# Late stages of an attention and gated-unit backward kernel: VectorE in program order, input-gradient rows ended over two head groups, O*wo rows reordered

## The chip, the cores and the metric

The kernel runs on one core of a Trainium2 chip. The metric is device time in microseconds (us). The kernel before takes 4983.85 us, the median of four runs (4983.04 to 5001.55).

The engines are TensorE (PE in the profile; its weight loads are PEld), VectorE (DVE), ScalarE (ACT), GpSimd (POOL) and SyncE (SP). SP computes nothing: it issues transfers. POOL computes a little and issues the other transfers. Each engine works through its own list of instructions in order, and waits at an instruction until the semaphores it names have come.

## The reference

One forward pass and its gradients with respect to eight inputs. With S = 2048 rows, D = 576 columns, H = 32 heads of width 128, F = 4608:

```
xn  = layernorm(x)
q   = xn @ wq, per head;  p = softmax(q k^T / sqrt(128));  o = p v
s   = concat(o) @ wo
g   = silu( (sigmoid(xn @ w_gate) * (xn @ w_up)) @ w_down )
out = x + s * g
```

`jax.vjp` of this with a given `grad_out` yields the gradients of x, k, v, wq, wo, w_gate, w_up and w_down. Everything is bfloat16 in memory. The kernel writes nine outputs: `out` (out_0), the gradient of x (out_1), of k and v (out_2, out_3), wq (out_4), wo (out_5), w_gate, w_up (out_6, out_7) and w_down (out_8).

## The kernel before

Rows are handled in NT = 16 tiles of 128. A first part computes the layer norm, the gated unit and the silu, and attention walks over the heads, forward and backward. Both are untouched. Attention leaves in HBM the attention output (`on2_d`), the gradient of q (`dq2_d`), and, turned the wrong way round, the gradients of k and v (`kvT_d`). The gated unit left `a_d` (the sigmoid) and `h_d` (the product). What follows are the late stages, within one `tc.manual_schedule`. In it SP and POOL issue in the order of the program text. The instructions of TensorE, ScalarE and VectorE are put in an order ahead of the run by a planner, with estimated costs; at run time each engine follows its fixed list.

**O*wo.** For each of the 16 row tiles, `load_oT` (line 584, SP) brings the attention output of all heads in, transposed, to one of three places `oTs` (tiles KQ, xnT and xn_all in the profile). `mm(st, heads)` adds 32 heads' products with the rows of wo (line 957, TensorE). The wo rows lie in tiles that attention has finished with; three of these (Kn, Vn, dOn) become free last, and their heads are `h_late`, the others `h_early`. `close(st)` copies the sums out (ScalarE), multiplies by the loaded rows dsg and g2b and adds xb (VectorE, lines 969 to 972), stores out_0 (POOL) and asks for the row three further on. `turn_do(st)` turns the tile doB on TensorE (line 915) into doBT, through a PSUM tile and copies on ScalarE and VectorE. The first three rows run their early heads first, then the late heads of each.

**Blocks.** F is cut into 18 blocks of 256 columns (`for fb`). Two tiles, ah0 and ah1, hold a and h of this block and the next in turn (loads on POOL, line 895). The loop over row pairs computes dh = doB * w_down^T (line 1092, TensorE, two PSUM buffers). From dh come nbl = (a-1)*h (line 1093, VectorE; it needs only a and h), du_blk = dh*a (line 1094, VectorE), ndh = -dh (line 1096, ScalarE) and dg_blk = ndh*nbl (line 1097, VectorE). duT and dgT are turned by SP (line 1047). Then come six sums over all rows by `accumulate` (line 997): two for out_8 (copied to dwd by ScalarE) and two each for out_7 and out_6 (copied to dwT, turned by SP, line 1121). Last, for 16 rows, `dx_row` (line 1052) gives the block's share of the input gradient, which VectorE adds to dxn (line 1130).

**The k and v gradients** are turned along the way: `kv_turn` issues one 512 KB transpose on SP (line 1038) into one of two buffers kvn, `kv_store` its store on POOL (line 1044). There are 64 of them. The blocks do three each, so 54; the head groups do the rest.

**Head groups.** The 32 heads form eight groups of four (`for hg`). A group loads the next one's `onb` and `dqb` (POOL, lines 1026 and 1029), turns its slice of wq (SP, line 1179; the tile shares memory with wdT) and dqb (SP, into dqbT), and does four pairs of sums: for out_4 (copied to dqT, turned by SP, line 1202) and for out_5 (copied to dwo, line 40, stored by POOL, line 1209). Then `dx_more(st)` gives the group's share of the input gradient for each row, four products each, and VectorE adds it to dxn (line 1222). In the last group the rows are instead ended: `finish(st, acc)` does five VectorE operations (tot, junk, m, nb, t; lines 1156 to 1163), one ScalarE operation on t (line 1164), and on POOL the addition of `grad_out`'s row to give dx (line 1166) and its store. All 16 rows do this in the last group, spread between its sums from the second on. The sums share four PSUM buffers.

Of the kernel before, what the change touches and what calls it, by code (L numbers as in the profile page):

```python
# [9 lines left out]
bf = mybir.dt.bfloat16  # L10
f32 = mybir.dt.float32
# [55 lines left out]
def kernel(  # L67
# [814 lines left out]
    with late("pc") as pc, late("pcf") as pcf, \  # L882
            tc.manual_schedule(engines={mybir.EngineType.SP, mybir.EngineType.Pool}):
# [21 lines left out]
        with late("c1l3", 4) as ldp3, late("c1s", 2) as sb, \  # L905
# [4 lines left out]
            def turn_do(st):  # L910
                pt = pst.tile([P, 8, P], bf, name="pt", tag="tr")
# [27 lines left out]
            loads = {}  # L939
            for st in range(1, R0):  # L940
                load_oT(oTs[st], st)
            loads[0] = row_loads(0)
# [33 lines left out]
            for st in range(R0):  # L976
                mm(st, h_early)
            for st in range(NT):
# [5 lines left out]
                while len(pend_tr) > 1:  # L984
                    st_ = pend_tr.pop(0)
                    turn_do(st_)
                mm(st, h_late if st < R0 else h_early + h_late)
                close(st)
            for st_ in pend_tr:
                turn_do(st_)  # L990
# [66 lines left out]
        with late("b1b") as blk, late("b1t", 3) as tmpp, late("b1o", 2) as outp, \  # L1057
# [4 lines left out]
            kdw = 0  # L1062
            for fb in range(NFB):
# [22 lines left out]
                for st in range(0, NT, G2):  # L1086
                    sp_ = slice(st, st + G2)
                    dh = ps.tile([P, G2, FB], f32, name="dh")
# [4 lines left out]
                    nc.vector.scalar_tensor_tensor(nbl[:, sp_, :], a_blk[:, sp_, :], 1.0, h_blk[:, sp_, :], op0=ALU.subtract, op1=ALU.mult)  # L1093
# [5 lines left out]
                    if e % NTQ == 0:  # L1099
                        for k in range(2):  # L1100
                            turn_rows(dugT[k], dug[k], e - NTQ, e, FBT)
                kv_store()
# [3 lines left out]
                for fl in range(FBT):  # L1106
                    dwd = outp.tile([P, D], bf, name="dwd")
                    accumulate(psa.tile([P, WD], f32, name="acc"), h_blk, doB, slice(fl * P, (fl + 1) * P), dwd)
# [5 lines left out]
                for (blk_, out_, nm) in ((du_blk, out_7, "dwu"), (dg_blk, out_6, "dwg")):  # L1114
                    stg_ = outp.tile([P, DT, FB], bf, name=nm)
                    for fl in range(FBT):
# [3 lines left out]
                        accumulate(psa.tile([P, WD], f32, name="acc"), blk_, xn_all, lcols, dwT)  # L1120
                        nc.sync.dma_start_transpose(stg_[:, :, lcols], dwT[:])
                    store_T(out_, fcols, stg_)
                kv_turn(blk)
                for st in range(NT):
                    acc = psa.tile([P, WD], f32, name="acc")
# [3 lines left out]
                    else:  # L1129
                        nc.vector.tensor_tensor(dxn[:, st, :], acc[:, :D], dxn[:, st, :], op=ALU.add)  # L1130
                kv_store()

        with late("c2w") as wp, late("c2b") as blk, late("c2s", 2) as sb, late("c2ps", 4, space=PSUM) as ps:
            dqTs = padded(wp, 2, "dqT")
            onqs = [(onb0, dqb_at.get(0)), tuple(blk.tile([P, NT, HC], bf, name=nm)[:] for nm in ("onb", "dqb"))]
            if not dqb_at:
                onqs[0] = (onb0, carve(ah0[:], "p a t f -> p (a t f)", NT, HC))
                load_dq(onqs[0][1], 0)
            dqbT = blk.tile([P, NT * HG, P], bf, name="dqbT")

            def dx_more(st):
                acc = ps.tile([P, WD], f32, name="acc")
                dx_row(acc, st, [(dqbT[:, st * HG + hl, :], wqT[:, hl, :]) for hl in range(HG)])
# [112 lines left out]
```

## Time and profile before

| what | us |
|---|---|
| median of four runs | 4983.85 |
| the profiled execution's own time | 4995.39 |
| its span, first to last instruction | 4993.6 |
| TensorE busy in it | 4845.4 |
| VectorE busy | 2794.1 |
| ScalarE busy | 2475.6 |
| POOL busy | 864.5 |

The profiled execution is a single one and is 11.5 us above the median. Views of the profile give, for an instruction, its start and duration in us, the engine, the line of the kernel, the operation, what it writes and reads (out<-in), and in square brackets how long its engine was idle before it and what ended that wait. "SPq" stands for a transfer that SP issues; its duration there is that of the issue, and a merged row (x4) spans several. In the view of windows each engine's busy time in a stretch is followed by its number of instructions; the last three columns are the granted TensorE clock (1 is full), the busy share of the 16 DMA engines (which can exceed 1 where transfers overlap) and the GB moved per second. A row of waits names the waiting instruction, what it waited for, and the total, the number and the longest.

### The profile page before, as it was taken

The page shows a single profiled execution, that of the slowest core. Times are in us where ns is not written, and L with a number is a line of the kernel's source. Part 1 is how long each engine was busy: PE and PEld are TensorE (multiplying, and loading weights), DVE is VectorE, ACT ScalarE, POOL GpSimd, SP SyncE. Part 2 cuts the span into 40 slices and gives each one's busy share as a digit, 9 for nine tenths or more (in the row PEclk, how much of TensorE's full clock was granted, in tenths as well). Part 3 has the DMA queues.
Part 4 walks back from the last instruction along what each step waited for, and adds up shares of the span by engine and source line. Part 5 has one row for each costly group of instructions (what it writes and reads, how often), then busy time and mean ns, then how long its engine had stood idle before and what let it go on. Part 6 is the DMA issues. An engine that isn't in the chain of part 4 may idle for free.

```text
span 4993.6 us, 100884 instructions
## 1 busy us (share of the span) xinstructions
PE 4845.4 (97%) x40269; PEld 2895.8 (58%) x41029; DVE 2794.1 (56%) x6546; ACT 2475.6 (50%) x4228; POOL 864.5 (17%) x1344
## 2 busy tenths in 40 slices
PE   8999999999999999999999999999999999998998
PEld 4445666666666666666666666665555555554554
DVE  4544665666666666566566666666334545452225
ACT  4422766766766766766666676676221111111011
POOL 3322111111111111111111111111221111111113
PEclk9999999999999999999999999999999999999999
DMA  7887999999999999999999999999998889889974
GB/s 260 272 207 170 224 227 226 228 230 224 226 234 226 221 228 234 220 230 223 228 221 240 220 224 237 224 223 228 221 226 192 208 190 206 194 208 204 252 206 122
DMA packets 3045876, 1097.09 MB, mean 220 GB/s; under 512 B 2949585, under 2 KB 2953810, under 8 KB 3045394
## 3 DMA queue, kind: packets, MB, share of 16 engines
q1 hardware_dynamic: 2946626, 771.07, 82.3%
q0 software_dynamic: 98160, 318.85, 20.1%
q8 instruction: 322, 5.28, 0.4%
q14 instruction: 160, 1.31, 0.1%
q10 hardware_dynamic: 608, 0.59, 0.0%
HBM read 175.31 MB, written 177.93 MB: 71 GB/s over the span
## 4 chain that ended last, share of the span: by engine, by line
PE 85%; DMA 7%; DVE 3%; issue 2%; SPq 1%; POOL 1%; ACT 1%; DVEq 0%; POOLq 0%; ACTq 0%
PE acc L683 18%; PE acc L744 17%; PE acc L997 12%; PE dp L706 8%; PE sp L636 8%; PE acc L215 5%; DMA ah<-h_d 3%; PE acc L1052 3%; PE u_ps L450 3%; PE g_ps L448 3%; PE acc L533 2%; PE acc L957 2%; DMA kvn<-kvT_d 1%; DMA PT<-Pq 1%; PE acct L145 1%
## 5 line engine op out<-in xcount | busy, mean ns | idle before, releaser
L654 ACT ACTIVATE Pq<-sp 128x1024 bf16<-128x1024 f32 x1024 | 1047.0, 1023 | 270.5 <-PE sp L636 227.6
L709 DVE SCALAR_TENSOR_TENSOR Pq<-dp,negdelta,Pq 128x1024 bf16<-128x1024 f32 x512 | 654.8, 1279 | 42.9 <-PE dp L706 42.8
L712 ACT ACTIVATE t<-dp,negdelta 128x1024 bf16<-128x1024 f32 x512 | 567.2, 1114 | 215.5 <-PE dp L706 165.7
L683 PEld LDWEIGHTS <-dST 128*128 128x128 bf16 x8192 | 507.3, 98 | 148.9 <-DMA dST<-Pq 8.3
L706 PE MATMUL dp<-VT,dOT 128*128 128x512 bf16 x1919 | 581.2, 379 | 2.4
L683 PEld LDWEIGHTS <-PT 128*128 128x128 bf16 x8192 | 500.0, 98 | 142.0 <-DMA PT<-Pq 24.3
L636 PE MATMUL sp<-KQ 128*128 128x512 bf16 x1858 | 567.8, 379 | 2.2 <-ACT Pq L654 2.1
L683 PE MATMUL acc<-Kn,dST 128*128 128x128 bf16 x8192 | 556.3, 219 | 5.4 <-DMA dST<-Pq 3.3
L683 PE MATMUL acc<-Vn,PT 128*128 128x128 bf16 x8192 | 543.0, 219 | 17.2 <-DMA PT<-Pq 14.6
L744 PE MATMUL acc<-Pq,dOn 128*128 128x512 bf16 x1983 | 528.2, 379 | 10.2 <-issue 0.2
L713 DVE TENSOR_TENSOR Pq<-t,Pq 128x1024 bf16<-128x1024 bf16 x512 | 354.4, 692 | 313.2 <-ACT t L712 305.8
L744 PE MATMUL acc<-Pq,Qn 128*128 128x512 bf16 x2013 | 522.9, 379 | 5.0
L1130 DVE TENSOR_TENSOR dxn<-acc,dxn 128x576 f32<-128x576 f32 x272 | 206.0, 757 | 388.9 <-PE acc L1052 388.9
L724 ACT ACTIVATE dq_n<-acc,rsc 128x128 bf16<-128x128 f32 x512 | 187.5, 366 | 329.5 <-PE acc L683 308.0
L744 PEld LDWEIGHTS <-Qn 128*128 128x128 bf16 x2048 | 200.1, 98 | 240.0
L744 PEld LDWEIGHTS <-dOn 128*128 128x128 bf16 x2048 | 199.0, 98 | 234.5 <-issue 1.1
L1096 ACT ACTIVATE ndh<-dh 128x512 bf16<-128x512 f32 x144 | 86.0, 597 | 407.9 <-DVE du_blk L1094 407.8
L706 PEld LDWEIGHTS <-dOT 128*128 128x128 bf16 x2048 | 178.8, 98 | 124.5 <-issue 12.4
L636 PEld LDWEIGHTS <-KQ 128*128 128x128 bf16 x2048 | 179.0, 98 | 123.8 <-issue 3.1
L641 DVE TENSOR_REDUCE rs_all<-rsp 128x1 f32<-128x2 f32 x512 | 78.4, 153 | 306.3 <-ACT Pq L654 294.9
L677 POOL DMA_DIRECT2D on_d<-o_n x128 | 97.1, 759 | 793.0 <-DVE junk L695 460.0
L1222 DVE TENSOR_TENSOR dxn<-acc,dxn 128x576 f32<-128x576 f32 x112 | 84.8, 757 | 263.0 <-PE acc L1052 263.0
(206 smaller groups left out, 6834.5 us busy)
## 6 DMA issues: line engine op xcount, KB each, us to landing
out_dram<-kvn POOLq DMA_DIRECT2D x64, 512.0 KB, 4.5
ah<-a_d POOLq DMA_DIRECT2D x18, 1024.0 KB, 8.6
ah<-h_d POOLq DMA_DIRECT2D x18, 1024.0 KB, 10.9
h_d<-h_row POOLq DMA_DIRECT2D x64, 256.0 KB, 3.3
a_d<-a_row POOLq DMA_DIRECT2D x64, 256.0 KB, 3.7
x_all<-in_A_k_cache_dram SPq DMA_DIRECT2D x64, 256.0 KB, 3.6
on_d<-o_n POOLq DMA_DIRECT2D x128, 128.0 KB, 4.8
kvT_d<-KQ POOLq DMA_DIRECT2D x32, 512.0 KB, 4.9
```

What stands on the lines that cost most here:

```text
L215: nc.tensor.matmul(av[:, :CH], lhsT=w[:, i, :], rhs=srcT[:, i, cs], start=(i == 0), stop=(i == DT - 1))
L636: nc.tensor.matmul(sp[:, c * CH:(c + 1) * CH], lhsT=hs.QT[:, qt * P:(qt + 1) * P], rhs=hs.KT[:, hf * HW_ + c * CH: hf * HW_ + (c + 1) * CH ...
L654: nc.scalar.activation(Pq[:, hsl], sp[:], AF.Exp, scale=SCALE, accum_out=hs.rsp[:, hf:hf + 1])
L683: nc.tensor.matmul(hs.acc[:, 0, :], lhsT=T[:, kt, :], rhs=rhs[:, kt, :], start=(kt == 0), stop=(kt == NT - 1))
L706: nc.tensor.matmul(dp[:, c * CH:(c + 1) * CH], lhsT=hs.dOT[:, qt * P:(qt + 1) * P], rhs=hs.VT[:, hf * HW_ + c * CH: hf * HW_ + (c + 1) * C ...
L709: nc.vector.scalar_tensor_tensor(Pq[:, hsl], dp[:], hs.negdelta[:, qt:qt + 1], Pq[:, hsl], op0=ALU.add, op1=ALU.mult)
L712: nc.scalar.activation(t[:], dp[:], AF.Identity, bias=hs.negdelta[:, qt:qt + 1], scale=1.0)
L713: nc.vector.tensor_tensor(Pq[:, hsl], t[:], Pq[:, hsl], op=ALU.mult)
L724: nc.scalar.activation(hs.dq_n[:, qt % G4, :], hs.acc[:, 0, :], AF.Copy, scale=hs.rsc[:, qt:qt + 1])
L744: nc.tensor.matmul(self.acc, lhsT=self.nat[:, qt, :], rhs=self.slabs[qt][:, cs], start=(qt == self.lo), stop=(qt == self.hi - 1))
L997: nc.tensor.matmul(acc[:, n0:n0 + nn], lhsT=lhs[:, st, cols], rhs=rhs[:, st, n0:n0 + nn], start=(st == 0), stop=(st == NT - 1))
L1130: nc.vector.tensor_tensor(dxn[:, st, :], acc[:, :D], dxn[:, st, :], op=ALU.add)
```

## The change

VectorE joins SP and POOL in the list of engines that follow the program text. With that, the text itself is rearranged:

- **O*wo.** Row 0's loads come first. Before the transposes of rows 1 and 2, POOL copies one element from one of those loads (g2b for row 1, xb for row 2) into the target, so that the transpose waits for it. Two rows, not three, run their early heads ahead; row 2's follow the closing of row 0. The last turns of doB go to the next stage, into the loop of the first block, where they use a PSUM buffer of the sums.
- **Blocks.** nbl is computed within the loop only in the first block; otherwise it is made for the next block behind the loop. A fourth kv transpose and store come per block: one transpose and one store behind the turns of dwu, one transpose behind those of dwg. A loop behind the blocks would do what is left.
- **Head groups.** They do no kv work. In the last but one group (`early`), the first eight rows are ended for both groups at once: they take eight products, four with dqbT and wqT and four with a second pair, dqbT2 and wqT2, turned from the last group's data. These rows are spread from that group's fourth sum on. Its other eight rows are added to dxn as before. The last group ends the other eight rows and turns only their part of dqb.
- **finish.** The addition of `grad_out`'s row moves from POOL to VectorE.

```diff
-            tc.manual_schedule(engines={mybir.EngineType.SP, mybir.EngineType.Pool}):
+            tc.manual_schedule(engines={mybir.EngineType.SP, mybir.EngineType.Pool, mybir.EngineType.DVE}):
...
-            def turn_do(st):
-                pt = pst.tile([P, 8, P], bf, name="pt", tag="tr")
+            def turn_do(st, pt):
...
+            loads[0] = row_loads(0)
             for st in range(1, R0):
+                nc.gpsimd.tensor_copy(oTs[st][0:1, 0, 0:1], loads[0][st % 3][0:1, 0:1])
                 load_oT(oTs[st], st)
-            loads[0] = row_loads(0)
...
-            for st in range(R0):
+            for st in range(R0 - 1):
                 mm(st, h_early)
...
-                mm(st, h_late if st < R0 else h_early + h_late)
+                mm(st, h_late if st in accs_of else h_early + h_late)
                 close(st)
-            for st_ in pend_tr:
-                turn_do(st_)
+                if st == 0 and R0 > 1:
+                    mm(R0 - 1, h_early)
...
+            def make_nbl(src, sl):
+                nc.vector.scalar_tensor_tensor(nbl[:, sl, :], src[:, 0, sl, :], 1.0, src[:, 1, sl, :], op0=ALU.subtract, op1=ALU.mult)
...
+                    while fb == 0 and pend_tr and (len(pend_tr) > 2 or st + 2 * G2 >= pend_tr[0]):
+                        turn_do(pend_tr.pop(0), psa.tile([P, WD // P * 2, P], bf, name="pt", tag="acc"))
...
-                    nc.vector.scalar_tensor_tensor(nbl[:, sp_, :], a_blk[:, sp_, :], 1.0, h_blk[:, sp_, :], op0=ALU.subtract, op1=ALU.mult)
+                    if fb == 0:
+                        make_nbl(ahb, sp_)
...
+                if fb + 1 < NFB:
+                    for st in range(0, NT, G2):
+                        make_nbl(nxt, slice(st, st + G2))
                 kv_store()
                 kv_turn(blk)
...
                     store_T(out_, fcols, stg_)
-                kv_turn(blk)
+                    kv_turn(blk)
+                    if nm == "dwu":
+                        kv_store()
...
+            while kv_left or kv_wait:
+                kv_turn(blk)
+                kv_store()
...
+            NTE = NT // 2 if NHG > 1 else 0
             dqbT = blk.tile([P, NT * HG, P], bf, name="dqbT")
+            dqbT2 = blk.tile([P, max(1, NTE) * HG, P], bf, name="dqbT2")
+            wqT2 = blk.tile([P, HG, D], bf, name="wqT2")
...
-            def dx_more(st):
+            def dx_more(st, both=False):
                 acc = ps.tile([P, WD], f32, name="acc")
-                dx_row(acc, st, [(dqbT[:, st * HG + hl, :], wqT[:, hl, :]) for hl in range(HG)])
+                terms = [(dqbT[:, st * HG + hl, :], wqT[:, hl, :]) for hl in range(HG)]
+                if both:
+                    terms += [(dqbT2[:, st * HG + hl, :], wqT2[:, hl, :]) for hl in range(HG)]
+                dx_row(acc, st, terms)
...
-                nc.gpsimd.tensor_tensor(dx[:], t[:], gots.pop(st)[:], op=ALU.add)
+                nc.vector.tensor_tensor(dx[:], t[:], gots.pop(st)[:], op=ALU.add)
...
+                early = hg == NHG - 2
+                ends = list(range(NTE)) if early else list(range(NTE, NT)) if final else []
...
-                if not final:
-                    kv_turn(blk)
                 nc.sync.dma_start_transpose(wqT, A_wq[:, cols])
-                for a in range(0, NT, NQ):
-                    turn_rows(dqbT, dqb, a, a + NQ, HG)
+                for a in range(NTE if final else 0, NT, NQ):
+                    turn_rows(dqbT, dqb, a, min(a + NQ, NT), HG)
+                if early:
+                    nc.sync.dma_start_transpose(wqT2[:], A_wq[:, (hg + 1) * HC:(hg + 2) * HC])
+                    turn_rows(dqbT2, onqs[(hg + 1) % 2][1], 0, NTE, HG)
...
+                wait_n = min(4 if early else 2, nsteps - 2)
+                todo_rows = list(ends)
...
+                def ends_rows():
+                    if todo_rows and step_n >= wait_n:
+                        for _ in range(-(-len(todo_rows) // max(1, nsteps - step_n - final))):
+                            if todo_rows:
+                                st = todo_rows.pop(0)
+                                finish(st, dx_more(st, early))
+                                if st + 2 <= ends[-1]:
+                                    load_got(st + 2)
...
-                    kv_store()
-                    for st in range(NT):
+                    for st in range(len(ends), NT):
                         acc = dx_more(st)
                         nc.vector.tensor_tensor(dxn[:, st, :], acc[:, :D], dxn[:, st, :], op=ALU.add)
-            while kv_left or kv_wait:
-                kv_turn(blk)
-                kv_store()
+                while todo_rows:
+                    step_n = nsteps
+                    ends_rows()
```

## The prediction

> **What bounds the kernel now.** I read the shares first, then the late stages as windows, the waits in them, and the timeline at each long wait.
>
> ```profile
> PE 4845.4 (97%) x40269; PEld 2895.8 (58%) x41029; DVE 2794.1 (56%) x6546; ACT 2475.6 (50%) x4228; POOL 864.5 (17%) x1344
> ```
> TensorE (PE) sets the time: a gain has to come from its idle time, about 148 us of the span. Attention (to about 3536 us) is not edited. The windows of the rest are, in order: O*wo, all feed-forward blocks, head groups 0, 1 and 6, and the last group, 7.
>
> ```profile
> core 0: us, PE busy (x) PEld busy (x) DVE busy (x) ACT busy (x) POOL busy (x), PEclk, DMA share, GB/s
> 3535.80:3676.00 140.20, 131.28 (x1078) 69.74 (x1100) 36.97 (x61) 17.78 (x45) 38.88 (x69) 0.98 0.92 215
> 3676.00:4570.20 894.20, 862.80 (x7061) 507.11 (x7204) 439.03 (x708) 166.44 (x272) 140.13 (x203) 1.00 0.87 204
> 4570.20:4636.00 65.80, 49.35 (x379) 25.32 (x386) 12.12 (x17) 4.91 (x8) 11.25 (x17) 0.87 1.08 217
> 4871.20:4918.00 46.80, 46.38 (x375) 24.26 (x382) 12.07 (x16) 5.10 (x8) 4.59 (x8) 1.00 0.49 112
> 4918.00:4993.60 75.60, 52.34 (x379) 26.09 (x384) 56.05 (x114) 18.40 (x24) 43.85 (x52) 0.85 0.48 119
> ```
> The same matmuls take 46.8 us in group 6, 65.8 us in group 0 and 75.6 us in group 7, where the halved clock shows too (0.87, 0.85). The blocks idle for 31 us. The waits of these stages:
>
> ```profile
> ACT dqT L40 <- DMA dwq<-dqT: 37.0, 2, 30.2
> DVE nbl L1093 <- DMA ah<-h_d: 22.8, 15, 5.0
> PE dh L1092 <- ACT ndh L1096: 22.2, 31, 4.8
> PE acc L1052 <- ACT dqT L40: 15.9, 1, 15.9
> ```
> Lines two and three are one event: VectorE waits for the next block's load ahead of nbl, and du_blk, ndh and dh stand behind it. Lines one and four are group 0: TensorE waits for the copy dqT, and that for a transpose queued on SP.
>
> **Part 1, blocks: nbl out of the loop, VectorE in program order.** One step of the loop, in the timeline of block 8:
>
> ```profile
> 4126.43 0.69 DVE L1094 TENSOR_TENSOR du_blk<-dh,ah 128x512 bf16<-128x512 f32 x1 [0.33 <-PE dh L1092]
> 4127.22 0.60 ACT L1096 ACTIVATE ndh<-dh 128x512 bf16<-128x512 f32 x1 [16.92 <-DVE du_blk L1094]
> 4128.13 0.41 DVE L1097 TENSOR_TENSOR dg_blk<-ndh,nbl 128x512 bf16<-128x512 bf16 x1
> ```
> ndh starts 0.1 after du_blk ends. Start to start, I summed what exceeds a matmul's columns at 2.4 GHz by over 0.3: 29.7 us over blocks 1 to 17, 5.2 of it in block 1, which also pays 1.7 for a halved clock (3735.4 to 3738.8). Block 17 has no next nbl to make, and waits 0.52. Hence a bound: 29.7 - 17 x 0.52 + 1.7 = 22.5 us.
>
> What program order takes back: dg_blk now stands between two du_blk, so a step costs VectorE 0.69 + 0.1 + 0.60 + 0.1 + 0.42 = 1.9, and eight 15.2 us; block 17's run of dh took 10.4. TensorE has 8.8 us of dh (80 matmuls at 0.11) plus 7.8 of dwd (two sums of 3.92) to fill it: 16.6, just enough. The copies' waits double at most, from 0.5 to 1.0 a block: gain 29.7 - 17 + 1.7 = **14.4**. Ends: 22.5 gained; 57 lost if the fill is not used (a rival below). The eight nbl (5.5 us) follow at about +15 to +21 us in a block, after its load has landed (4131 in this block, +6), and VectorE's next work is the dxn sums at +34: hidden, with 13 us of slack.
>
> **Part 2, kv copies: four a block in blocks 0 to 15, none after.** Each moved copy issues a 512 KB transpose on SP and a store on POOL. From the packet records a block moves 5.56 MB through transposes in 30.8 us of the 16 engines' time and 4.2 MB of the other transfers in 12.5. A further copy adds 2.9 + 1.6 = 4.5, so 48.1 of a 49.4 us block. It fits if it falls in a hole: the transpose goes between dwu's and dwg's on SP, at about 4154, and nearly nothing moves from 4154 to 4156 and 4158 to 4161. The new store waits on POOL for its transpose (median 5.2 to landing) ahead of dwg's store and the next block's loads; these have the slack of part 1. Cost taken: **0**; without that cover 1 us a block, 16.
>
> Blocks 16 and 17 and the groups lose this traffic. The gain is in group 0:
>
> ```profile
> 4546.52 10.87 SPq L1038 DMA_TRANSPOSE kvn<-kvT_d  x1
> 4565.49 6.04 SPq L1038 DMA_TRANSPOSE kvn<-kvT_d  x2
> 4571.57 8.36 SPq L1179 DMA_TRANSPOSE wdT<-in_A_wq_dram  x1
> 4580.04 34.19 SPq L1047 DMA_TRANSPOSE dqbT<-ah  x4
> ```
> Four dqbT took 34.2 us here and 9.4 at 4874, in group 6. Without the 10.9 and 6.0 ahead of it, the wq transpose moves from 4571.6 to about 4558. dqbT then cannot start before the blocks' last row (4570) frees memory; at 181 KB a us its 2 MB take 11.6, plus 12.8 while the 4 MB for group 1 load: done by 4595. TensorE needs it at 4602. Group 0 could fall by 65.8 - 47.1 = 18.7; I take **17**, ends 0 and 18.7.
>
> **Part 3, the end.** Half the rows move to group 6.
>
> ```profile
> 4931.92 1.82 POOL L1166 TENSOR_TENSOR dx<-t,got 128x576 bf16<-128x576 f32 x1 [4.29 <-ACT t L1164]
> 4932.52 1.84 DVE L1157 SCALAR_TENSOR_TENSOR junk<-tot,xn_all 128x576 f32<-128x576 f32 x1
> ```
> A junk beside POOL's add takes 1.84 instead of 0.76 (mean 1.21). The Trainium skill, "SBUF — State Buffer", Who interferes with whom, says why: VectorE with two SBUF inputs and a reading GpSimd exclude each other. By that rule alone the move to VectorE pays: 16 rows took 4927.1 to 4983.2, 3.5 each, and tot + junk + m + nb + t + add unhindered is 0.76 + 0.76 + 0.16 + 0.15 + 0.81 + 0.76 = 3.4. But the rule leaves out the order: the new add waits for ScalarE's t (0.1 + 0.87 + 0.1) and the next row's tot stands behind it, so the row costs **4.45**, eight 35.6. I take that.
>
> Group 6 starts at 4871.2. It gains eight rows of 1.96 in place of eight of 0.98: 47.1 + 7.8 = 54.9 for TensorE. VectorE starts the rows after four sums (15.7) and a row (2), ends them at +53.3, and adds the other eight (0.76 each) as sums come: TensorE, with four sum buffers, ends near +58. SP now carries wq2 (2.9) and a 1 MB dqbT2 (about 5) ahead of dwq's four transposes: dqbT2 lands near 4894, and the first row wants it at 4887. I take 3 of these 7 us, since the order may put other sums first; ends 0 and 8. Group 7 then starts at 4932.2. TensorE has 31.4 + 7.8 = 39.2, VectorE starts at +9 and ends at +44.6; dx, dwq and dwo stores stand on POOL (2.5), then 5.4 us as after POOL's last issue now (4988.2 to 4993.6): +52.5, 4984.7. Gain **9**, ends 18 gained and 5 lost.
>
> **Part 4, O*wo.** Two tiny POOL copies now hold the oT transposes of rows 1 and 2 until row 0's g2b and xb have landed.
>
> ```profile
> 3532.81 5.34 SPq L584 DMA_TRANSPOSE xnT<-on_d  x1
> 3542.62 2.56 PE L957 MATMUL acc<-dsT,KQ 128*128 128x512 bf16 x10 [4.15 <-issue]
> 3543.40 0.55 POOL L934 DMA_DIRECT2D dsg<-dsg_d  x1 [6.65 <-issue]
> 3570.09 2.10 PE L957 MATMUL acc<-dsT,KQ 128*128 128x512 bf16 x15 [3.25 <-DMA KQ<-on_d]
> ```
> SP ran ahead: row 1's transpose went out at 3532.8 and its sums began at 3548.2 without a wait. Now it waits for g2b, issued at 3543.95 (2.5 to land, as got does alone; 10 in this crowd). So: g2b 3546.5, copy and signal 3546.9, oT1 in 8.2 more (KQ, 3561.9 to 3570.1): 3555.1, against 3548.2, **6.9** idle. Row 2's lands at 3560.4, in time; the three late wo loads behind the copies on POOL land near 3556.5, in time for the new order.
>
> The skill's "TensorE: Matmul & The Clock Gate", Part 1, speaks against the change here: after an idle window of about 3.4 us the array runs at half clock, until it has been busy as long. The rows agree with a rule of about that size: the idle of 4.15 halved the clock from 3540.8 to 3547.6, that of 3.25 at 3570 didn't. By the rows of waits alone 6.9 is all; by the rule some 2.5 more (half-speed work over 3.4 to 6.8 us, an estimate). I add it. In return row 0 closes before row 2 starts, so row 3's transpose is early and the 3.4 at 3570 goes; the deferred turns save the 0.5 at the stage's end (their ten matmuls merely move). Sum: **5.5 lost**; ends 2 gained and 9 lost (the upper end if g2b takes its 10 us).
>
> **Sum.** 14.4 + 17 + 9 - 5.5 = 34.9 gained: the profiled execution's 4995.4 (span 4993.6 and 1.8 around it) becomes 4960.5. It lies 11.5 above the median shown, 4983.85, and I carry the difference over: **4949**.
>
> **Rivals.** *A, VectorE's order becomes the bound: slower.* If the fill of TensorE's waits stays as written for before (about 1.5 us of dwd per loop), the 15.2 us loop leaves 15.2 - 8.8 - 1.5 = 4.9 idle per block, 1.75 a block now: +3.2 x 18 = 57 lost where 14.4 were gained: 5020. For it: TensorE's order is fixed ahead, and ndh's chain is real. Against: blocks 16 and 17 waited only 0.8 and 0.5, though dh already waited on ndh there. It turns the sum at 2.1 us more idle per block than foreseen (34.9 / 17).
>
> *B, the fourth kv copy isn't hidden.* With 48.1 of 49.4 us of transfers a late kvn delays loads and dgT; 1 us over 16 blocks and the block gain gone is 30 less: 4979. Against: the holes above.
>
> *C, the change doesn't do what it says at the end.* dqbT2 late by all 8 us, TensorE cold after it (group 7 is at 0.85 now) and VectorE at 4.45 a row: no gain there, 4958.
>
> *D, group 0 keeps its stall*, because the onb and dqb loads of group 1 and not kv slow dqbT: 17 less, 4966. For it: these 4 MB were in flight in 4573 to 4595; against: in groups 1 to 6 four dqbT take 9 us.
>
> *E, all edits reach their good end*: 22.5 + 18.7 + 15 - 0 = 56: 4928.
>
> **How the numbers follow.** Mine 0.41 (own range 4938 to 4962), A 0.17, B 0.08, C 0.12, D 0.10, E 0.12. About 0.3% (15 us, 4969 to 4999) is what a measurement of this kernel can tell from no change. Faster: mine, C, D and E less 0.03 of D's that ends short: 0.72. Same: B, that 0.03 and 0.02 of A: 0.13. Slower: 0.15. The range of 8 in 10 leaves out 0.05 below and 0.15 of A above: 4924 to 4990.
>
> **What would show it.** Right: du_blk, ndh, dg_blk strictly in turn, near 1.9 us a step, with dwd matmuls between, and no nbl waiting ahead of du_blk; blocks of 48.5 to 49; no kvn after block 15; group 0 at 47 to 50 us and four dqbT in under 20; one add per row on VectorE behind t, the last group near 52; an idle of some 7 us before row 1 of O*wo with a halved clock after it. Wrong: blocks above 50 us with dh waiting for ndh (A) or DMA (B); a long dqbT in group 0 (D); TensorE waiting for dqbT2 or tot in group 6 (C).

## The result, and the profile after

Over 61 runs of the kernel before and 40 of the changed one on the same chips, the medians are 4990.11 us (4974.9 to 5020.47) and 4976.88 us (4964.18 to 4995.43). The ratio of the two kernels is 0.9971, with a 95% interval of 0.9963 to 0.9979: 14.5 us faster, 10.5 to 18.5 by the interval (the medians themselves differ by 13.2). The direction is the one forecast; the size is two fifths of the 34.9 us forecast. It is 0.29%, clear of zero by the interval and just short of the 0.3% that the prediction took for the least it could tell from no change. The median lies inside the forecast's range (4924 to 4990) and above the likeliest case's own (4938 to 4962).

The profiled execution of the changed kernel took 4975.24 us, with a span of 4973.4. From its page, the line of TensorE:

```profile
PE 4854.7 (98%) x40276; PEld 2896.2 (58%) x41029; DVE 2789.7 (56%) x6554; ACT 2476.1 (50%) x4228; POOL 842.9 (17%) x1330
```

By these sums TensorE idles for 118.7 us instead of 148.2. Both are too high, since some 750 of its 41029 matmuls have no record in these two profiles. The second profiles, below, have all of them: 92.4 before, 89.1 after. What a stage takes is therefore read from start times.

The same five windows as before (O*wo, all blocks, head groups 0, 6 and 7; columns as there: length, busy time of PE, PEld, DVE, ACT and POOL, then clock, DMA share, GB/s):

```profile
3537.50:3687.50 150.00, 132.09 (x1073) 69.80 (x1095) 36.87 (x60) 17.99 (x46) 39.35 (x71) 0.94 0.89 201
3687.50:4574.90 887.40, 872.85 (x7073) 507.02 (x7209) 444.48 (x708) 164.34 (x271) 149.12 (x218) 1.00 0.95 220
4574.90:4621.90 47.00, 46.63 (x378) 24.19 (x384) 12.08 (x17) 5.01 (x8) 7.01 (x9) 1.00 0.96 246
4857.10:4921.60 64.50, 56.67 (x443) 29.04 (x448) 31.68 (x73) 11.94 (x16) 12.12 (x22) 0.95 0.58 141
4921.60:4973.40 51.80, 39.34 (x315) 20.31 (x320) 26.94 (x66) 11.70 (x16) 11.03 (x20) 0.92 0.47 112
```

O*wo became 9.8 us longer (140.2 to 150.0), the blocks 6.8 shorter (894.2 to 887.4), group 0 is back at 47 (from 65.8), and groups 6 and 7 together take 116.3 instead of 122.4. The waits of the late stages, where the four long ones stood:

```profile
ACT dqT L40 <- DMA dwq<-dqT: 10.9, 1, 10.9
...
DVE nbl L1065 <- DMA ah<-h_d: 4.3, 1, 4.3
...
PE acc L1052 <- DMA dqbT<-dqb: 5.5, 1, 5.5
```

nbl's wait fell from 22.8 to 4.3. TensorE's waits for ndh (22.2) and for the copy dqT (15.9) are no longer among the listed ones; its wait for dqbT is that for the second pair in group 6.

One profile of each kernel turned out to be a thin basis. I therefore had both kernels profiled a second time, unchanged. The stages by TensorE's start times, in us, measured between the first matmuls of each stage, so that they differ from the windows by a few tenths (forecast: the prediction's gain or loss for the stage):

| stage | before | before, again | after | after, again | mean change | forecast |
|---|---|---|---|---|---|---|
| up to the end of attention | 3535.9 | 3538.7 | 3537.5 | 3535.8 | -0.7 | 0 |
| O*wo | 140.4 | 139.5 | 150.0 | 143.4 | +6.7 | +5.5 |
| block 0 | 48.4 | 48.4 | 49.1 | 49.1 | +0.7 | 0 |
| blocks 1 to 17 | 845.6 | 852.6 | 838.3 | 845.4 | -7.3 | -14.4 |
| of these, block 17 | 48.7 | 48.7 | 49.3 | 56.4 | +4.2 | |
| group 0 | 65.6 | 48.1 | 47.0 | 56.9 | -4.9 | -17 |
| groups 1 to 5 | 235.2 | 235.2 | 235.2 | 235.2 | 0 | 0 |
| groups 6 and 7 | 122.6 | 122.7 | 116.2 | 116.6 | -6.3 | -9 |
| span | 4993.6 | 4985.2 | 4973.4 | 4982.5 | -11.5 | -34.9 |

The change in the means, -11.5, lies inside the interval of the ratio (-10.5 to -18.5); the first pair alone would say -20.2.

### The profile page after: what moved, and what is told of

Read it like the earlier page. It is cut to its first block, busy times and chain, and to the rows that moved or that the text cites. A ratio compares the mean times of both kernels' runs of the same rounds, so it can differ in the third digit from the quotient of the medians.

```text
span 4973.4 us, 100870 instructions
## 1 busy us (share of the span) xinstructions
PE 4854.7 (98%) x40276; PEld 2896.2 (58%) x41029; DVE 2789.7 (56%) x6554; ACT 2476.1 (50%) x4228; POOL 842.9 (17%) x1330
## 4 chain that ended last, share of the span: by engine, by line
PE 88%; DVE 4%; issue 3%; DMA 3%; ACT 2%; SPq 1%; POOL 0%; ACTq 0%; POOLq 0%; DVEq 0%
PE acc L683 18%; PE acc L744 17%; PE acc L997 11%; PE sp L636 8%; PE dp L706 8%; PE acc L1052 7%; PE acc L215 5%; PE u_ps L450 3%; PE g_ps L448 3%; PE acc L533 2%; PE acc L957 2%; DVE du_blk L1101 1%; PE acct L145 1%; ACT ndh L1103 1%; PE dh L1098 1%
## 5 line engine op out<-in xcount | busy, mean ns | idle before, releaser
L683 PEld LDWEIGHTS <-dST 128*128 128x128 bf16 x8192 | 507.9, 98 | 154.3 <-DMA dST<-Pq 13.7
L1142 DVE TENSOR_TENSOR dxn<-acc,dxn 128x576 f32<-128x576 f32 x272 | 206.1, 758 | 305.5 <-PE acc L1052 305.5
L677 POOL DMA_DIRECT2D dq_d<-dq_n x128 | 98.2, 767 | 721.5 <-ACT dq_n L724 681.7
```

Of the source, the lines that this page charges most:

```text
L683: nc.tensor.matmul(hs.acc[:, 0, :], lhsT=T[:, kt, :], rhs=rhs[:, kt, :], start=(kt == 0), stop=(kt == NT - 1))
```

## The experiments

Each is compared with runs of the kernel before on its own chip, and the ratios below are to those, with 95% intervals. The chips differ (medians of before: 5005.4, 4993.8 and 4996.7), so runs of different chips are compared by their ratios.

| run | median us | ratio to before |
|---|---|---|
| both kernels again: before | 4987.03 (one run) | |
| both kernels again: after | 4977.83 | 0.9962 (0.9948 to 0.9977) |
| after without the POOL copies | 4957.97 | 0.9914 (0.9891 to 0.9938) |
| after with O*wo as before | 4968.89 | 0.9930 (0.9904 to 0.9955) |
| after, VectorE ordered by the planner | 4991.99 | 0.9985 (0.9968 to 1.0002) |
| before, VectorE in program order alone | 4978.33 | 0.9966 (0.9950 to 0.9981) |
| after, next du_blk ahead of dg_blk | 4964.94 | 0.9944 (0.9924 to 0.9965) |
| after, ndh ahead of du_blk | 4963.52 | 0.9944 (0.9926 to 0.9963) |
| after with kv copies as before | 4990.43 | 0.9980 (0.9962 to 0.9997) |
| after with the end as before | 4983.65 | 0.9986 (0.9973 to 0.9998) |
| no copies, ndh ahead | 4953.43 | 0.9911 (0.9894 to 0.9928) |
| the same, each row's addition later | 4950.14 | 0.9909 (0.9891 to 0.9926) |

### Both kernels again

No edit to either.

> The kernel before once more, for a second profile. The profile shown had an idle of 4.15 us on TensorE in O*wo that was put down to nothing (issue), the profile after had 3.6 us before a dST transpose in attention instead and none in O*wo. If that idle is chance, O*wo takes 131 to 134 us here instead of 140.4, and the edits of O*wo cost 16 to 19 us, not 9.6. If it belongs to the kernel before, O*wo takes 140 again and the edits cost 9.6. Blocks 1 to 17: 845 to 847 in both; head groups 423 in both.

> The changed kernel once more, beside the next three on the same chip. O*wo 150 to 154 us (150.0 in its first profile), blocks 1 to 17 838.3, groups 398 to 399, groups 6 and 7 together 116; ratio 0.996 to 0.998. If O*wo is at 143 or less, its waits are as much chance as edit.

The second profile of before has group 0 at 48.1, not 65.6, with all kv copies in place. The second profile of after has 56.9 there, and 56.4 in block 17, with none in place. The stall that the forecast wanted to remove is thus not a fixed cost of the kernel before, and not absent from the one after. The timeline of SP at that place, first in the second profile of before, then in the first of after (start, length of the issue, what it turns):

```profile
4570.34 21.60 SPq L1038 DMA_TRANSPOSE kvn<-kvT_d  x2
4591.99 5.79 SPq L1179 DMA_TRANSPOSE wdT<-in_A_wq_dram  x1
4597.88 10.20 SPq L1047 DMA_TRANSPOSE dqbT<-ah  x4
```
```profile
4567.81 3.03 SPq L1201 DMA_TRANSPOSE wdT<-in_A_wq_dram  x1
4575.17 24.40 SPq L1047 DMA_TRANSPOSE dqbT<-ah  x4
```

Some transpose is slow between about 4570 and 4614 in all three profiles: two kvn in this one (21.6), dqbT in after (24.4) and dqbT in the first profile of before (34.2). Which one it is goes with what stands on SP while the 4 MB for group 1 load. Without kvn in the queue dqbT is issued in full 24.6 us after group 0 starts; with it 28.9 in this profile and 44.0 in the first. TensorE asks for it after its four pairs of sums, at about 31. So the copies took a part of the reserve, and whether that shows is decided from execution to execution. In group 1 of the first profile of after, the loads for group 2 are issued at 4609.4 and 4610.6 and landed by 4623.8, ahead of the four dqbT at 4625.8, and these take 8.7: slow transposes and large loads stand together, which is no proof that the loads slow them.

### O*wo: without the copies, and with the stage as before

```diff
 for st in range(1, R0):
-    nc.gpsimd.tensor_copy(oTs[st][0:1, 0, 0:1], loads[0][st % 3][0:1, 0:1])
     load_oT(oTs[st], st)
```

> The changed kernel without its two POOL copies in O*wo; the new order of the rows stays. Theory: the copies are what costs there, since they put the transposes of rows 1 and 2 behind row 0's loads and the late wo loads ahead of them: O*wo falls from 150.0 to 131 to 135 us, ratio to before about 0.993. Rival (the new row order is what costs: row 0's late heads now stand ahead of row 1's early ones on TensorE and wait for the late wo rows): O*wo stays above 140, ratio 0.996 to 0.997. Blocks and groups as in the changed kernel, 838 and 398.

The second takes back the row order as well:

```diff
-loads[0] = row_loads(0)
 for st in range(1, R0):
     load_oT(oTs[st], st)
+loads[0] = row_loads(0)
...
-for st in range(R0 - 1):
+for st in range(R0):
     mm(st, h_early)
...
-    if st == 0 and R0 > 1:
-        mm(R0 - 1, h_early)
```

> The changed kernel with O*wo as before in its order and loads (three rows' early heads first, no copies); only the deferred turns stay. Theory and rival both: O*wo at 131 to 140; ratio to before 0.992 to 0.994 when the copies or the order cost 10 to 16 us. If the whole of O*wo costs nothing (the 9.6 us were chance), the ratio stays 0.997. Against the run without copies: equal if the copies alone cost, 5 us or more faster if the row order costs too.

The stage took 136.5 without the copies and 143.6 with copies and order undone (the deferred turns stay), against 150.0 and 143.4 with the copies. In the changed kernel the timeline shows the path of row 1's transpose and the waits of TensorE:

```profile
3541.93 0.54 POOL L933 DMA_DIRECT2D g2b<-g_d  x1
...
3544.68 0.18 POOL L941 COPY xnT<-g2b 1x1 bf16<-1x1 bf16 x1 [1.68 <-DMA g2b<-g_d]
3544.89 4.93 SPq L584 DMA_TRANSPOSE xnT<-on_d  x1
...
3547.11 0.74 POOL L575 DMA_DIRECT2D dOn<-in_A_wo_dram  x1
...
3549.91 14.52 SPq L584 DMA_TRANSPOSE xn_all<-on_d  x1
...
3555.26 1.60 PE L957 MATMUL acc<-Kn,KQ 128*128 128x512 bf16 x6 [11.57 <-DMA Kn<-in_A_wo_dram]
...
3562.25 6.22 PE L957 MATMUL acc<-dsT,xnT 128*128 128x512 bf16 x33 [3.06 <-DMA xnT<-on_d]
```

The copy waits for g2b as foreseen (2.75 from g2b's issue to the copy). But TensorE waits first for Kn, a late row of wo, for 11.57: its list holds row 0's late heads ahead of row 1's early heads. And row 1's transpose, issued at 3544.89, is used 17.4 later, not 8.2: it runs beside the row loads and the three wo loads. In between the clock is halved: the granted clock is 0.50 from 3550 to 3566. With the copies out, of all this one wait remains in the timeline of TensorE,

```profile
3532.22 2.70 PE L956 MATMUL acc<-dsT,KQ 128*128 128x512 bf16 x14 [4.50 <-issue]
```

and with the order of before there are two:

```profile
3548.53 3.52 PE L956 MATMUL acc<-dsT,KQ 128*128 128x512 bf16 x14 [5.02 <-issue]
...
3576.70 6.01 PE L956 MATMUL acc<-dsT,KQ 128*128 128x512 bf16 x34 [3.65 <-DMA KQ<-on_d]
```

So the two halves of this part pull apart. The new row order gains some 3 to 7 us, by the wait for KQ that disappears, as the sum had it (3.4). In the four profiles with the old order this wait was 2.74 to 3.68; behind the two longest, 3.65 here and 3.68, the next matmuls took 6.01 instead of 4.33, at a clock that was halved in part, which is another 1.7. The copies lose more than that: 142.9 to 153.9 in the seven profiles of kernels that have them (mean 149.6), 136.5 to 136.8 in the three that have the order without them.

By its ratio (0.9914 against 0.9971) the run without copies gained 28 us on the changed kernel; the intervals allow some 12 to 44, so the stage's 13 lie at their edge. Its profile also left attention 12 us sooner, which no edit touches; the rest isn't explained. A later run, on one chip with the changed kernel, had the copies out and one more step worth 8 to 9 us, and gained 24.4 by its median: about 16 for the copies.

### Blocks: program order and nbl, each alone

```diff
-with tc.manual_schedule(engines={SP, Pool, DVE}):
+with tc.manual_schedule(engines={SP, Pool}):
```

> The changed kernel with VectorE left to the planner; nbl behind the loop, kv copies and the end as changed. Theory: the program order (du_blk, then ndh on ScalarE, then dg_blk, a chain of 1.75 us a step) is what holds blocks at 49.31 us; with du_blk of the next step allowed ahead of dg_blk a block falls to 48.5 to 48.8, blocks 1 to 17 to 825 to 830, 9 to 13 us less. Rival: the blocks are at their floor by TensorE alone, 49.3 in both. Second rival: the planner puts nbl ahead again and waits for the load as before: 49.5.

The converse is the kernel before with VectorE put into that list and nothing else changed.

> The kernel before with VectorE in program order and nothing else changed, so nbl of a block stands ahead of du_blk in the block's own loop. Theory: program order takes away the wait for the next block's load, but the step is then nbl, du_blk, ndh, dg_blk one after the other, 0.69 + 1.75 = 2.4 us a step and 19.5 a loop, more than the 16.6 us with which TensorE fills it: blocks 51 to 53 us, slower than before by 20 to 60 us. Rival: nbl falls into VectorE's wait for dh or ndh, the step stays at 1.75 to 1.9 and the block at 49.3 as with the changed kernel; then the order alone makes the gain and moving nbl none.

With the planner back, block 1 took 65.8 and blocks 1 to 16 on average 50.9, not the 48.5 to 48.8 expected. It pulls the next block's nbl, placed behind the loop in the text, back into the loop. In the timeline of VectorE:

```profile
4214.13 0.42 DVE L1104 TENSOR_TENSOR dg_blk<-ndh,nbl 128x512 bf16<-128x512 bf16 x1
4218.59 0.69 DVE L1065 SCALAR_TENSOR_TENSOR nbl<-ah 128x512 bf16<-128x512 bf16 x1 [4.04 <-DMA ah<-h_d]
4219.20 0.42 DVE L1104 TENSOR_TENSOR dg_blk<-ndh,nbl 128x512 bf16<-128x512 bf16 x1
```

That is the stall of the kernel before, and larger (38.2 us of waits for h_d, against 22.8). Program order is therefore what keeps nbl out of the way. Alone on the kernel before it makes nearly every block 49.6 us, where the planner's order varied from 48.7 to 54.8. The expected 51 to 53 did not come. One step takes 2.36 us, as that sum had it, but TensorE's list fills it with eight dwd matmuls, where the changed kernel has four:

```profile
4223.20 0.69 DVE L1093 SCALAR_TENSOR_TENSOR nbl<-ah 128x512 bf16<-128x512 bf16 x1
...
4223.97 1.14 PE L997 MATMUL acc<-doB,ah 128*128 128x64 bf16 x8
...
4225.56 0.69 DVE L1093 SCALAR_TENSOR_TENSOR nbl<-ah 128x512 bf16<-128x512 bf16 x1
```

With nbl moved as well a block is 49.31: nbl's place is worth 0.28 a block, 5 us in all. The run with the order alone is 18 us faster than before, about as much as all parts of the change together.

### Blocks: the order within a step

In the changed kernel one step, in the timeline of block 8, is strictly du_blk, ndh, dg_blk, 1.75 us a step (1.9 was forecast), with four dwd matmuls between the runs of dh:

```profile
4236.33 0.68 DVE L1101 TENSOR_TENSOR du_blk<-dh,ah 128x512 bf16<-128x512 f32 x1
...
4237.09 0.65 PE L997 MATMUL acc<-doB,ah 128*128 128x64 bf16 x4
4237.10 0.60 ACT L1103 ACTIVATE ndh<-dh 128x512 bf16<-128x512 f32 x1 [1.15 <-DVE du_blk L1101]
...
4237.73 0.43 DVE L1104 TENSOR_TENSOR dg_blk<-ndh,nbl 128x512 bf16<-128x512 bf16 x1 [0.72 <-ACT ndh L1103]
4237.75 1.25 PE L1098 MATMUL dh<-wdT,doBT 128*128 128x256 bf16 x10
...
4238.08 0.68 DVE L1101 TENSOR_TENSOR du_blk<-dh,ah 128x512 bf16<-128x512 f32 x1
```

dh starts 0.05 after ndh ends, since ndh is the last reader of its PSUM buffer. The list of waits doesn't show this: the modelled end of the dwd matmuls reaches up to dh. But matmuls of 512 and 64 columns follow each other in 217 and 28 ns here (448 columns in 189 ns, the 2.4 GHz of the prediction's count). The four dwd matmuls (two of 512 columns, two of 64) thus need 0.49 us, and 0.66 pass from their start to that of dh: 0.17. In block 8 of the second profile, which has every record, six of the eight runs of dh start 0.17 to 0.39 late in this way, 1.4 us in all. Two runs shorten this chain in different ways. One puts dg_blk behind the next step's du_blk, so that du_blk does not wait for ndh:

```diff
-nc.vector.tensor_tensor(dg_blk[:, sp_, :], ndh[:], nbl[:, sp_, :], op=ALU.mult)
-(turn_rows for this step)
+behind.append((ndh, sp_, st + G2))
+while len(behind) > (1 if st + G2 < NT else 0):
+    (the oldest step's dg_blk, then its turn_rows)
```

> The changed kernel with dg_blk of a step written behind du_blk of the next step; all else as changed. Theory: VectorE's fixed order du_blk, dg_blk costs the ndh wait (0.72 us) at every step, the step takes 1.75 us, and TensorE's dh waits about 0.2 us a step for ndh. With the next du_blk in that hole a step falls to about 1.4, blocks from 49.31 to 48.5 to 48.8, blocks 1 to 17 from 838.3 to 825 to 830; ratio to before 0.994 to 0.995. Rival: TensorE's fill with dwd hides it already, and 49.31 stays.

The other changes the order of the two readers of dh:

```diff
-nc.vector.tensor_tensor(du_blk[:, sp_, :], dh[:], a_blk[:, sp_, :], op=ALU.mult)
 ndh = ... nc.scalar.mul(ndh, dh, -1.0)
+nc.vector.tensor_tensor(du_blk[:, sp_, :], dh[:], a_blk[:, sp_, :], op=ALU.mult)
```

> The changed kernel with the ndh copy written ahead of du_blk, so that ScalarE reads dh first and VectorE after it. Theory: dg_blk follows du_blk without a wait (1.1 us a step on VectorE, ndh of the next step runs beside it), dh's two buffers set 1.35 to 1.4 a step, blocks fall to 48.5 to 48.8 as with du_blk ahead. Rival: the two reads stay one behind the other either way, dh's buffer is free no sooner, and the block stays at 49.3.

Blocks took 48.82 and 48.79 instead of 49.31, all alike: 8 to 9 us in all (13 by both ratios, whose intervals hold the 8 to 9). With ndh first, three runs of dh a block start late instead of six, by 0.29 each (read in block 8 of the later run that has this order and every record). With ndh first, ScalarE starts as soon as dh is there, and VectorE is the last reader:

```profile
4226.44 0.60 ACT L1102 ACTIVATE ndh<-dh 128x512 bf16<-128x512 f32 x1 [1.02 <-PE dh L1098]
...
4227.07 0.69 DVE L1103 TENSOR_TENSOR du_blk<-dh,ah 128x512 bf16<-128x512 f32 x1 [0.60 <-ACT ndh L1102]
...
4227.53 0.60 ACT L1102 ACTIVATE ndh<-dh 128x512 bf16<-128x512 f32 x1 [0.49 <-PE dh L1098]
4227.68 0.41 DVE L1104 TENSOR_TENSOR dg_blk<-ndh,nbl 128x512 bf16<-128x512 bf16 x1
```

### The kv copies as before

```diff
-kv_turn(blk)
-if nm == "dwu":
-    kv_store()
...
+kv_turn(blk)   # once a block, behind both turns
... (and the groups' turns and stores put back)
```

> The changed kernel with the kv copies as before: three a block, the other ten in the head groups. Theory of the prediction: the two kv transposes near the border and the stores delay wq and dqbT, and group 0 stalls again, 60 to 66 us instead of 47.0; ratio to before 0.999 to 1.0. Rival (the stall of the first profile of before was chance, or a matter of when the block before it ends; the second profile of before had 48.1): group 0 at 47 to 50, all else as changed, ratio 0.997. Blocks stay at 49.31 by both, which would show that the fourth copy is hidden.

Blocks 1 to 16 took 49.31 with three copies as with four: the fourth is hidden. In this profile block 17 took 56.2 and group 0 53.8, which is 13.7 above the first profile of after; but the second profile of after, without copies there, has the same two stalls, 17.0 above. The timeline of that one shows what is slow in block 17:

```profile
4530.35 1.16 POOL L1115 DMA_DIRECT2D doBT<-ds_d  x1 [22.27 <-PE dh L1098]
...
4537.07 1.17 POOL L1026 DMA_DIRECT2D doB<-on_d  x1
...
4537.99 20.73 SPq L1047 DMA_TRANSPOSE dgT<-dg_blk  x1
...
4561.70 0.73 PE L1052 MATMUL acc<-wug,duT 128*128 128x512 bf16 x4 [2.63 <-DMA duT<-du_blk]
4564.00 1.14 PE L1052 MATMUL acc<-wug,dgT 128*128 128x512 bf16 x4 [1.57 <-DMA dgT<-dg_blk]
```

The last dgT takes 20.7 us beside the large loads for the groups, where its like earlier in the block takes 1.86, and dwu's and dwg's transposes queue behind it. TensorE waits 4.2 us for duT and dgT, and the matmuls behind run at the halved clock (1.15 for four instead of 0.66), which together is nearly the 7. In the first profile of after the dgT took 13.5 and just didn't show.

By the ratios (0.9980 against 0.9971) the run is 4 us slower than the changed kernel, and the intervals overlap. The 14 profiles of this study say more, since their code at this place differs in little but the copies. With the copies in the groups (four profiles) group 0 took 48.1 to 65.6, on average 55.1. Without them (ten) it took 47.0 to 47.5 in eight and 55.9 and 56.9 in two, on average 49.0. Block 17 took 55.3 to 59.6 in one of the four and in three of the ten. With both counted, the move is worth about 5.5 us.

### The end as before

```diff
-NTE = NT // 2 if NHG > 1 else 0
+NTE = 0
-nc.vector.tensor_tensor(dx[:], t[:], gots.pop(st)[:], op=ALU.add)
+nc.gpsimd.tensor_tensor(dx[:], t[:], gots.pop(st)[:], op=ALU.add)
-early = hg == NHG - 2
+early = False
```

> The changed kernel with the end as before: all 16 rows ended in the last group, grad_out's row added on POOL; VectorE still in program order. Groups 6 and 7 together took 122.6 us in both profiles of before and 116.2 in the changed one. Theory: the new end is worth those 6 to 7 us, and more here, since VectorE's program order no longer mixes two rows' chains: a row costs 2.64 us and the waits [...], 4 us in all, so groups 6 and 7 take 122 to 132 us; ratio 0.998 to 1.000. Rival: the gain of 6 us is VectorE's order alone, and the groups take 116.

Groups 6 and 7 took 123.3: this part is worth 7. A row costs VectorE 3.62 there, from 4924.76 to 4928.38, though no junk is stretched: POOL's addition now falls on m instead.

```profile
4925.55 0.76 DVE L1179 SCALAR_TENSOR_TENSOR junk<-tot,xn_all 128x576 f32<-128x576 f32 x1
4925.83 1.62 POOL L1188 TENSOR_TENSOR dx<-t,got 128x576 bf16<-128x576 f32 x1 [0.61 <-ACT t L1186]
...
4926.36 1.12 DVE L1181 TENSOR_SCALAR m<-cs 128x2 f32<-128x2 f32 x1
```

### The gains together

The first takes out the copies and puts ndh first, both as above.

> The changed kernel without the two POOL copies and with the ndh copy ahead of du_blk: the two single steps that gained, together. If they add: O*wo 133 to 137 us, blocks 1 to 17 829, groups 398; 22 us less than the changed kernel, ratio to before 0.988 to 0.991. If they don't add (what is won in O*wo is lost in block 0, or the reverse): 0.992 or more.

The second also puts a row's addition and store behind the next row's five operations:

```diff
-nc.vector.tensor_tensor(dx[:], t[:], gots.pop(st)[:], op=ALU.add)
-nc.gpsimd.dma_start(o1[st * P:(st + 1) * P, :], dx[:])
+ended.append((st, t, dx))
...
     finish(st, dx_more(st, early))
+    add_rows(1 if todo_rows else 0)   # the additions and stores of all but the last
```

> As the run with both steps together, and in the ended rows the addition of grad_out's row (with its store) is put behind the next row's five VectorE operations. Theory: VectorE's row falls from 4.45 us (it waits about 1.0 for ScalarE's t) to 3.4 to 3.5, groups 6 and 7 together from 116 to 107 to 111 us. Rival: TensorE's own 94 us, the transposes for the last group and the stores set these groups, and they stay at 114 to 116.

O*wo took 136.6 and 136.8, blocks 48.79, though block 17 stalled in both profiles (59.6 and 55.3). Groups 6 and 7 fell from 116.7 to 109.7 with the later addition. In the timeline of VectorE in the last group, the changed kernel,

```profile
4952.44 0.75 DVE L1178 SCALAR_TENSOR_TENSOR tot<-acc,dxn 128x576 f32<-128x576 f32 x1
...
4954.31 0.81 DVE L1185 SCALAR_TENSOR_TENSOR t<-xn_all,m,tot 128x576 f32<-128x576 bf16 x1
4956.11 0.76 DVE L1188 TENSOR_TENSOR dx<-t,got 128x576 bf16<-128x576 f32 x1 [0.99 <-ACT t L1186]
4956.79 0.75 DVE L1178 SCALAR_TENSOR_TENSOR tot<-acc,dxn 128x576 f32<-128x576 f32 x1
```

and the last run, where no wait stands ahead of dx:

```profile
4918.14 0.75 DVE L1177 SCALAR_TENSOR_TENSOR tot<-acc,dxn 128x576 f32<-128x576 f32 x1
...
4920.01 0.81 DVE L1184 SCALAR_TENSOR_TENSOR t<-xn_all,m,tot 128x576 f32<-128x576 bf16 x1
4920.74 0.75 DVE L1194 TENSOR_TENSOR dx<-t,got 128x576 bf16<-128x576 f32 x1
4921.41 0.75 DVE L1177 SCALAR_TENSOR_TENSOR tot<-acc,dxn 128x576 f32<-128x576 f32 x1
```

A row, from tot to tot, falls from 4.35 to 3.27 us. The last version, 4950.14, is the best of the study: 46.6 us below before and 27.7 below the changed kernel in the same batch. The medians of the two versions differ by 3.3, less than the stage's 7; their intervals overlap, so the 7 is the profile's.

## Why the prediction was right in direction and wrong in size

**Part 1, blocks: the mechanism right, one term too small.** The order of a step, the place of nbl (its wait fell to 4.3), the even blocks and the use of dwd as fill came as written, so rival A, which left that fill unused, did not happen. The sum allowed the copies' waits 1.0 us a block. Without the idle counted in it and without block 1's slow clock, before's block is (845.6 - 29.7 - 1.7) / 17 = 47.9; the changed block is 49.31. The term is thus 1.4, and 17 times the 0.4 are the 7 us by which this part fell short in the first pair of profiles (7.3 instead of 14.4). What the term lacked is that dh waits 0.17 to 0.39 for ndh at six of the eight steps; the two runs that shorten the step take 0.5 a block away.

**Part 2, kv copies: hidden in the blocks, right; 17 us in group 0, wrong as a forecast.** In the first pair group 0 did fall by 18.6. But the 17 was read from one execution. The second profile of before had 48.1 with the copies in place, so there was 1 to gain there; and after's second profile had 56.9. Over the two pairs 4.9 are left, about 6 over all 14 profiles, and one of after's two profiles loses 7 in block 17 instead. Two steps failed. The 65.8 was taken for a fixed cost of the kernel before. And the sum for dqbT, 11.6 + 12.8 = 24.4 us, "done by 4595", was taken for certain: the four took just that in the first profile of after (which the sign "under 20" had overlooked), but 35.8 in the second, with no kvn ahead of them in either. There they were issued in full 36.0 after group 0 started, and TensorE asks at 31. Rival D's cause, the large loads, is the one that the profiles point to (in before these 4 MB were in flight until 4604, not 4595); D's conclusion, that group 0 keeps its stall, held in one of two, and in two of ten. Rival B did not happen: the fourth copy cost nothing (its 48.1 us of transfers a block add up to 47.8). What makes these loads and transposes collide in one execution and not in the next stays open.

**Part 3, the end: right, with one term too small.** The row on VectorE cost 4.35, forecast 4.45, because it waits for t as said; dqbT2 was ready 22.4 us into group 6, forecast 22.8. Group 7 took 51.8, forecast 52.5. Group 6 took 64.5, forecast 61. In the timeline of TensorE:

```profile
4879.55 2.10 PE L1052 MATMUL acc<-wqT,dqbT 128*128 128x512 bf16 x8 [5.51 <-DMA dqbT<-dqb]
...
4917.71 4.08 PE L1052 MATMUL acc<-wdT,dqbT 128*128 128x512 bf16 x32 [1.68 <-DVE dxn L1242]
```

The choice of 3 of the 7 us of dqbT2, "since the order may put other sums first", was the wrong one: the order put no other sum first, and TensorE waited 5.5, with eight matmuls behind it at the halved clock (2.10 instead of 1.15). VectorE then ended its rows at +59.8 instead of +53.3, and held a sum buffer for 1.7. Together this gave 6.3 instead of 9. Of rival C, no gain at the end, the first cause was thus there, at two thirds of its size.

**Part 4, O*wo: wrong.** The forecast of 5.5 is close to the mean of two profiles (+6.7), but by luck: not for its reasons, and five of the seven profiles with the copies show 150 to 154 (mean 149.6, against 141.5 in the four with the old order and no copies). Two steps failed. "The three late wo loads ... in time for the new order": the first, Kn, landed at 3555.3 and the next, Vn, at 3558.1, near the 3556.5 forecast, but TensorE's list wanted them ahead of row 1, from 3543.7 on. I had kept the order of the text for TensorE, whose order the planner makes. And "oT1 in 8.2 more" was taken from a transpose in a quieter place; in this crowd it was 17.4. The wait for g2b itself was right, and so was the clock's part: the halved clock cost at least (1.60 - 0.90) + (6.22 - 4.33) = 2.6, counted against matmuls of the same kind at 3576.42 and 3581.39, forecast 2.5. The waits for KQ fit the rule that it used (an idle of about 3.4 us) as well: behind 2.74 and 3.25 the clock stayed full, behind 3.65 and 3.68 it fell. But in block 17 it fell behind two waits of 2.63 and 1.57 with 0.7 us of work between them (granted clock 0.50 from 4564 to 4569). The return of 3.4 came too, as the run without copies shows. The idle of 4.15 "issue" at the start of before's stage was not chance: all seven profiles without the copies have it, at 3.5 to 5.0 us, and none of the seven with them (0.6 at most). What makes it stays open.

**The sum.** With the mean changes of the table in place of the four terms it is +6.7 + 0.7 - 7.3 - 4.9 - 6.3 = -11.1, against -11.5 between the spans and -14.5 by the ratio. Of the 23 us missing to the 34.9, about half is Part 2's reading of one execution, and 7 is the blocks: in the first pair the step alone; in the second the kernel before took 7 longer in blocks 1 to 16, which made up for the step, and block 17 lost 7. The rest is Part 3's 3 and Part 4's 2.

The base was off as well: the median of before is 4990.11 over 61 runs, 6.3 above the one over four runs from which 4949 was counted. (Rival E's 15 and 0 are not the good ends of Parts 3 and 4, which were 18 and 2.) The best version shows that some 28 us more lay in the same places: 13 in the copies, 8 to 9 in the order of ndh and du_blk, 7 in the addition.

## What to carry to other kernels

A stall seen in one profile is one draw: profile the kernel a second time before counting the stall's whole length as a gain. When an engine is put into program order, write down its chain per step with every reader of each PSUM buffer, and let the reader that another engine depends on go first. A transfer that is made to wait should be costed in the crowd it will then run in, and against the order that the consumer's list really has.

## What the runs showed of the hardware that was not expected

- The issue of a transpose varies far more than assumed, and the slow ones stand beside large loads. One of the same size took 1.86 and 20.7 us (dgT, block 17), row transposes of O*wo 4.6 later in the stage and 14.5 beside the wo and row loads, two kvn 6.0 and 21.6.
- POOL's addition stretches a very small operation of VectorE as well: m, 128x2, took 1.12 us beside it (it ended as the addition did) and 0.17 in the changed kernel. The loss is not bounded by the operation's own length.
- Executions of one program spread over 45 us (4975 to 5020 for before). In the 14 profiles here attention, the same code in all, ended between 3525.1 and 3552.4 us.
